# Storing the attention rows of a block in three parts of two chunks, through two half-size buffers

## The chip, the cores and the metric

The kernel runs on one core of a Trainium2 chip. The metric is the time of one execution in microseconds (us), read from the device. Five engines work side by side, each through its own program in order: PE (matrix multiplies; its weight loads are listed as PEld), DVE (vector), ACT (activations, and here also copies out of the matmul banks), POOL, and SP, which here only issues transfers. Transfers run on 16 DMA engines that all issuing engines share. Matmuls write into PSUM banks; another engine must copy ("evict") a bank before it can be written anew.

## The reference

What must be computed, cut to its core:

```python
# q, k, v: (4, 12, 448, 64); w_pre, w_post: (12, 12)
scores = scale * (q @ k.T)                       # per batch and head
scores = einsum('bhij,hg->bgij', scores, w_pre)  # mix of the heads
attn = exp(scores - max); attn /= sum + 1e-9
attn = einsum('bhij,hg->bgij', attn, w_post)     # second mix
x = (attn @ v) as rows of 768                    # 1792 rows
out = (sigmoid(x @ w_gate) * (x @ w_val)) @ w_out
```

Everything is float32. The first half (attention) makes x, the second half (a gated layer of width 1536) uses it.

## The kernel before, in words

Attention goes by blocks of 120 query rows (88 in the last block of a batch): 4 blocks in each of 4 batches, 16 in all. A block has sets of ten rows; two sets make a unit, and one unit is worked on in one **slot** of the main loop. There are 92 units, six to a block of 120 and five to a block of 88. Several units are in flight: in slot s the first mix (`premix`, line 213, PE) and the maximum (`rowmax`, line 218, DVE) are done for unit s+3, the exponential (`expo`, line 225, ACT) too, the scaling (lines 231, 237 and 243, on DVE and POOL) for unit s+1, and the second mix (`postmix`, line 255, PE, evicted by `mix`, line 263, ACT) for unit s. The scores of a later block (line 159, PE, evicted at line 165) run in between. `premix` reads a tile T that `regroup` (lines 203 and 205) loads six slots ahead, from SP; there are four T buffers and three `pm` banks, and a bank is free again when `expo` has read it.

When a block's second mix is complete, `av` (line 282, PE) multiplies it with v. The result has six chunks of 128 columns by the block's rows. Chunks 0 and 1 are made in the slot after the block, chunks 2 and 3 two slots later, chunks 4 and 5 four slots later, each at the slot's end. They go to one PSUM bank (pool `ps_av`, one buffer). After chunk 3, ACT evicts four chunks at once into `xt` (line 292), and after chunk 5 the last two. Pool `xp` holds a single `xt` buffer of four chunks, so an eviction into it waits until the store before it has landed. The stores are issued by `flush` (line 271) at the start of the next slot, on SP, right behind that slot's `regroup`. SP also issues the loads of k, q and v (lines 137, 145 and 172) and of raw weights for the second half (line 1037). SP's transfers take eight completion semaphores in turn, so each one waits until the transfer eight places ahead of it has landed.

The last two blocks differ: chunks 4 and 5 of the last block but one go into a spare T buffer, and the last block's six chunks are all made in one slot and evicted into the `mix` buffer that is then free, chunks 4 and 5 by way of the `mx` bank. After that the second half loads x from DRAM (line 1107) and works on its own order, which a planner fixes when the program is built; the planner doesn't know of the evictions.

Of the kernel before, what the change touches and what calls it, by code (L numbers as in the profile page):

```python
# [9 lines left out]
F32 = mybir.dt.float32  # L10
# [6 lines left out]
AF = mybir.ActivationFunctionType  # L17
# [7 lines left out]
QB = 120  # L25
# [16 lines left out]
def _attention(ctx, tc, ins, B, H, S, D, xs, raws, make_moe):  # L42

    nc = tc.nc
# [3 lines left out]
    KC = H * D // 128  # L48
# [7 lines left out]
    const = ctx.enter_context(tc.tile_pool(name="a_const", bufs=1))  # L56
    vst = ctx.enter_context(tc.tile_pool(name="a_vst", bufs=3))
    mp = ctx.enter_context(tc.tile_pool(name="a_m", bufs=1))
    xp = ctx.enter_context(tc.tile_pool(name="a_x", bufs=1))
    grp_ctx = ExitStack()  # L60
    tp, ep, pp, sm = (grp_ctx.enter_context(tc.tile_pool(name=f"a_{n}", bufs=b))
                          for n, b in (("t", 1), ("e", 3), ("p", 2), ("s", 4)))
# [6 lines left out]
    ps_av = ctx.enter_context(tc.tile_pool(name="ps_av", bufs=1, space=PSUM))  # L69
    ps_mx = ctx.enter_context(tc.tile_pool(name="ps_mx", bufs=1, space=PSUM))  # L70
# [6 lines left out]
    def two_banks(pool, tag):  # L77
        return pool.tile([128, 2, 512], F32, tag=tag, name=tag)
# [11 lines left out]
    sw = const.tile([128, 1], F32, name="sw")  # L90
# [35 lines left out]
    NU = len(units)  # L126
    moe = make_moe(NG)
    NBK = len(blocks)
# [39 lines left out]
    vt = {}  # L168
# [22 lines left out]
    mixes = [mp.tile([128, 4, H, QB], F32, name=f"mix{i}") for i in range(2)]  # L191

    t_bufs = [tp.tile([128, 2, S], F32, name=f"T{i}") for i in range(4)]
# [73 lines left out]
    av_t, stores = {}, []  # L267

    def flush():
        while stores:  # L270
            nc.sync.dma_start(out=stores[0][0], in_=stores.pop(0)[1])

    def av(bi, c):
        b, i0, n = blocks[bi][:3]
        u, h = divmod(2 * c, QUAD)
        if c % 4 == 0:
            last = bi == NBK - 1 and c
            t = two_banks(ps_mx, "mx")[:, 0] if last else ps_av.tile([128, 512], F32, tag="av", name="av")
            av_t[bi] = t[:, :4 * QB].rearrange("p (c s) -> p c s", c=4)
        for jb in range(4):  # L280
            for i in range(2):
                nc.tensor.matmul(av_t[bi][64 * i:64 * i + 64, c % 4, :n], lhsT=vt[b, u][:, h + i, jb, :],  # L282
                                 rhs=mixes[bi % 2][:, jb, 2 * c + i, :n], start=(jb == 0), stop=(jb == 3))
        if c % 4 == 3 or c == KC - 1:
            c0 = c - c % 4
            if bi == NBK - 1:
                xt = mixes[1 - bi % 2][:, c // 4, :4][:, :c + 1 - c0, :n]
            elif bi == NBK - 2 and c0:
                xt = t_bufs[NU % len(t_bufs)][:, 0, :(c + 1 - c0) * n].rearrange("p (c s) -> p c s", s=n)
            else:  # L290
                xt = xp.tile([128, 4, QB], F32, tag="xt", name="xt")[:, :c + 1 - c0, :n]
            nc.scalar.activation(out=xt, in_=av_t.pop(bi)[:, :c + 1 - c0, :n], func=AF.Copy, scale=sw)
            stores.append((xs[b, c0:c + 1, :, i0:i0 + n].rearrange("c p s -> p c s"), xt))
            if bi == NBK - 1:
                flush()

# [14 lines left out]
    for b in range(B):  # L311
# [3 lines left out]
        s = f + 5  # L315
        for i in range(H // 2):
            s = max(s + 1, f + 6 + 2 * (2 * i // QUAD))
# [16 lines left out]
    for bi in range(NBK):  # L334
        s0 = first[bi + 1]
        s1 = first[bi + 2] if bi + 2 < len(first) else s0
        for c in range(KC):
            at(min(s0 + c // 2 * 2, s1), av, bi, c)
            if bi == NBK - 1:
                at(s1, moe.between, c)  # L340
# [63 lines left out]
    for s in range(min(min(plan), -LEAD), max(plan) + 1):  # L404
# [25 lines left out]
        if 0 <= s + 1 < NU:  # L430
            p_lo(s + 1)
        tail = (av, moe.between, moe.early)
        if s == NU - 1:
            nc.scalar.activation(out=iw, in_=sw, func=AF.Sigmoid)
# [774 lines left out]
@with_exitstack  # L1209
def kernel(ctx, tc, B, H, S, D, ins, out):  # L1210
    nc = tc.nc
    top = ctx.enter_context(tc.tile_pool(name="top", bufs=1))
    dram = ctx.enter_context(tc.tile_pool(name="dram", bufs=1, space=DRAM))
    xs = dram.tile([B, H * D // 128, 128, S], F32, name="xs")
    with tc.manual_schedule():
        raws = top.tile([128, 13 * H * D // 2], F32, name="raws")
        with ExitStack() as c2:
            moe = _attention(c2, tc, ins, B, H, S, D, xs, raws,
                             lambda NG: _Moe(tc, xs, ins, out, raws, NG, top))
        moe.run()  # L1220
# [72 lines left out]
```

## Time and profile before

| | us |
|---|---|
| median of three executions | 796.8 (796.78 to 797.81) |
| the profiled execution | 798.64 |
| its span, first to last instruction | 796.9 |
| PE busy in the span | 770.0 (97%) |
| ACT busy in the span | 566.9 (71%) |

Attention fills the span up to about 365 us; what follows is the gated layer. All rows come from the one profiled execution; its span, 796.9, is 1.7 us below its own time and stands at the median of the other executions. A matmul's end is modelled by the profile, so that a PE that shows no idle time can still be slowed by its clock; the granted clock, in parts of full speed, is listed with each stretch.

### The profile page before, as it was taken

The page shows a single profiled execution, that of the slowest core. Times are in us where ns is not written, and L with a number is a line of the kernel's source. Part 1 is how long each engine was busy: PE and PEld are TensorE (multiplying, and loading weights), DVE is VectorE, ACT ScalarE, POOL GpSimd, SP SyncE. Part 2 cuts the span into 40 slices and gives each one's busy share as a digit, 9 for nine tenths or more (in the row PEclk, how much of TensorE's full clock was granted, in tenths as well). Part 3 has the DMA queues.
Part 4 walks back from the last instruction along what each step waited for, and adds up shares of the span by engine and source line. Part 5 has one row for each costly group of instructions (what it writes and reads, how often), then busy time and mean ns, then how long its engine had stood idle before and what let it go on. Part 6 is the DMA issues. An engine that isn't in the chain of part 4 may idle for free.

```text
span 796.9 us, 23624 instructions
## 1 busy us (share of the span) xinstructions
PE 770.0 (97%) x9626; PEld 425.7 (53%) x9626; DVE 631.9 (79%) x1092; ACT 566.9 (71%) x1122; POOL 253.6 (32%) x426
## 2 busy tenths in 40 slices
PE   8999999999979999968999999999999999999998
PEld 2465666566646666654555555555555555555554
DVE  4996899799958998789998989679786899997111
ACT  3897989898968899777886867668766784563000
POOL 1563547454534455420213122223322222010000
PEclk9999999999989999979999999999999999999999
DMA  5776678747875475636615374665657788995001
GB/s 187 253 239 214 206 236 262 260 153 237 256 231 188 158 234 192 233 109 231 204 55 195 131 243 169 247 201 187 210 162 272 279 310 300 381 355 222 35 35 69
DMA packets 80716, 166.16 MB, mean 209 GB/s; under 512 B 20448, under 2 KB 57664, under 8 KB 80608
## 3 DMA queue, kind: packets, MB, share of 16 engines
q1 hardware_dynamic: 72304, 132.88, 50.3%
q0 software_dynamic: 7728, 31.27, 10.2%
q8 instruction: 75, 1.23, 0.6%
q10 hardware_dynamic: 576, 0.51, 0.2%
q14 instruction: 33, 0.27, 0.1%
HBM read 87.77 MB, written 38.15 MB: 158 GB/s over the span
## 4 chain that ended last, share of the span: by engine, by line
PE 80%; ACT 6%; DMA 5%; DVE 5%; POOL 2%; issue 1%; SPq 1%; ACTq 0%; DVEq 0%; POOLq 0%
PE bank L1147 32%; PE bank L1158 18%; PE pm L213 9%; PE qk L159 8%; PE av L282 7%; PE mx L255 6%; ACT e L225 2%; DVE m L1131 2%; ACT mix L263 2%; DMA T<-st 2%; DMA m<-xs 1%; DMA xs<-xt 1%; DVE pl L243 1%; DVE nm L218 1%; ACT st L165 1%
## 5 line engine op out<-in xcount | busy, mean ns | idle before, releaser
L1147 PEld LDWEIGHTS <-m 128*128 128x128 f16 x1512 | 147.5, 98 | 142.3 <-DVE m L1131 4.1
L1147 PE MATMUL bank<-m,m 128*128 128x448 f16 x1116 | 214.4, 353 | 3.3 <-DVE m L1131 3.2
L237 POOL TENSOR_SCALAR ph<-e,ss 128x448 f16<-128x448 f32 x180 | 112.6, 638 | 158.3 <-DVE ss L231 114.4
L225 ACT ACTIVATE e<-pm,nm 128x448 f32<-128x448 f32 x180 | 115.2, 641 | 30.3 <-DVE nm L218 27.9
L218 DVE TENSOR_REDUCE nm<-pm 128x1 f32<-128x448 f32 x180 | 103.3, 614 | 32.7 <-PE pm L213 29.5
L213 PE MATMUL pm<-T,w 64*64 64x448 f32 (+1 forms) x720 | 110.1, 564 | 7.8 <-ACT e L225 5.4
L243 DVE SCALAR_TENSOR_TENSOR pl<-e,ss,ph 128x448 f16<-128x448 f32 x180 | 115.8, 683 | 2.0 <-POOL ph L237 2.0
L1158 PEld LDWEIGHTS <-m 128*128 128x128 f16 x756 | 73.9, 98 | 69.1
L159 PE MATMUL qk<-k,q 64*64 64x448 f32 x736 | 103.8, 549 | 3.2 <-ACT st L165 2.0
L263 ACT ACTIVATE mix<-mx 128x960 f32<-128x960 f32 (+1 forms) x92 | 104.4, 1135 | 1.5 <-PE mx L255 1.5
L255 PEld LDWEIGHTS <-ph 64*128 64x128 f16 x2880 | 64.5, 94 | 72.1 <-issue 40.3
L1158 PE MATMUL bank<-m,m 128*128 128x448 f16 x468 | 92.9, 353 | 0.0
L282 PE MATMUL av<-mix,v 128*64 128x120 f32 (+1 forms) x1504 | 86.0, 269 | 0.0
L255 PE MATMUL mx<-w2hi,ph 64*128 64x60 f16 x1440 | 72.2, 190 | 7.0 <-ACT mix L263 5.2
L1147 PE MATMUL bank<-m 128*128 128x448 f16 x396 | 77.9, 353 | 0.1
L282 PEld LDWEIGHTS av<-mix,v 128*64 128x64 f32 x1504 | 76.0, 141 | 2.7 <-issue 0.4
L255 PE MATMUL mx<-w2hi,pl 64*128 64x60 f16 x1440 | 71.4, 189 | 0.5 <-DVE pl L243 0.5
L255 PE MATMUL mx<-w2lo,ph 64*128 64x60 f16 x1440 | 71.3, 189 | 0.0
L1084 POOL CAST raws<-raws 128x768 f16<-128x768 bf16 x28 | 31.0, 1108 | 119.9 <-ACT raws L1078 119.7
L1078 ACT ACTIVATE raws<-raws 128x768 int16<-128x768 int8 (+1 forms) x72 | 60.1, 835 | 10.8 <-POOL raws L1084 10.6
L165 DVE COPY st<-qk 120x448 f32<-120x448 f32 (+1 forms) x92 | 56.5, 614 | 11.5 <-PE qk L159 11.5
L1174 DVE TENSOR_TENSOR m<-bank,m 128x448 f32<-128x448 f32 x72 | 44.5, 620 | 23.8 <-PE bank L1147 15.6
(127 smaller groups left out, 1056.7 us busy)
## 6 DMA issues: line engine op xcount, KB each, us to landing
T<-st SPq DMA_DIRECT2D x176, 210.0 KB
m<-w SPq DMA_DIRECT2D x60, 384.0 KB
raws<-in_w_dram SPq DMA_DIRECT2D x28, 767.6 KB
hs<-m POOLq DMA_DIRECT2D x48, 224.0 KB, 3.0
m<-hs SPq DMA_DIRECT2D x15, 672.0 KB
w<-m POOLq DMA_DIRECT2D x21, 384.0 KB, 4.5
w<-raws POOLq DMA_DIRECT2D x20, 384.0 KB, 4.7
v<-in_vb_dram SPq DMA_DIRECT2D x12, 512.0 KB
```

Of the source, the lines that this page charges most:

```text
L159: nc.tensor.matmul(sc[e][s0:s1, :S], lhsT=q[c][rows, s0:s1], rhs=k[rows, :], start=True, stop=True)
L165: (nc.vector.tensor_copy if e else nc.scalar.copy)(st_t[bi][:n, 2 * c + e], sc[e][:n, :S])
L213: nc.tensor.matmul(pm[bank][64 * x:64 * x + 64, :S], lhsT=w1[rows], rhs=T[rows, x], start=True, stop=True)
L218: nc.vector.tensor_reduce(nm[:, i:i + 1], pm[bank][:, :S], axis=AX.X, op=ALU.max, negate=True)
L225: nc.scalar.activation(out=e_t[u][:, i], in_=pm[units[u][2][i]][:, :S], func=AF.Exp, bias=nm_t[u][:, i:i + 1], scale=1.0, accum_out=ss_t[u ...
L237: nc.gpsimd.tensor_scalar(ph[:, i], e_t[u][:, i], ss_t[u][:, i:i + 1], 1.0, op0=ALU.mult, op1=ALU.mult)
L243: nc.vector.scalar_tensor_tensor(pl[:, i], e_t[u][:, i], ss_t[u][:, i:i + 1], p_t[u][0][:, i], op0=ALU.mult, op1=ALU.subtract)
L255: nc.tensor.matmul(mx[:, x, i, jb * HK:(jb + 1) * HK], lhsT=p[rows, i, JB[jb]:JB[jb] + 128], rhs=w[rows], start=(k == 0), stop=(k == 2))
L263: nc.scalar.activation(out=out.rearrange("p g (y r) -> p y g r", r=HALF), in_=mx_t.pop(u), func=AF.Copy, scale=1.0 / (P_UP * W_UP))
L282: nc.tensor.matmul(av_t[bi][64 * i:64 * i + 64, c % 4, :n], lhsT=vt[b, u][:, h + i, jb, :], rhs=mixes[bi % 2][:, jb, 2 * c + i, :n], start ...
L1147: self.nc.tensor.matmul(self.f32(bank), lhsT=w[a][:, k], rhs=x[b][:, k], start=self.START[i] and k == r == 0, stop=k == self.KH - 1 and r ...
L1158: self.nc.tensor.matmul(self.f32(bank), lhsT=w[a][:, k], rhs=b[bb], start=self.START[i] and j == k == r == 0, stop=j == OUT_TILES - 1 and ...
```

## The change

Each block is evicted three times, two chunks at a time, as soon as the two are made. Pool `xp` has two buffers of two chunks instead of one of four; the bytes are the same, and so is the space. The spare T buffer is no longer used for the last block but one. The last block takes chunks 2 and 3 as well by way of `mx`, one of its two banks each for chunks 2 and 3 and for 4 and 5. Evictions become 48 instead of 32, stores too; each has half the rows of chunks of the large one before.

```diff
-    xp = ctx.enter_context(tc.tile_pool(name="a_x", bufs=1))
+    xp = ctx.enter_context(tc.tile_pool(name="a_x", bufs=2))
...
-        if c % 4 == 0:
+        if c % 2 == 0:
+            if bi == NBK - 1 and c == 2:
+                av_t["last"] = two_banks(ps_mx, "mx")
             last = bi == NBK - 1 and c
-            t = two_banks(ps_mx, "mx")[:, 0] if last else ps_av.tile([128, 512], F32, tag="av", name="av")
-            av_t[bi] = t[:, :4 * QB].rearrange("p (c s) -> p c s", c=4)
+            t = av_t["last"][:, c // 2 - 1] if last else ps_av.tile([128, 512], F32, tag="av", name="av")
+            av_t[bi] = t[:, :2 * QB].rearrange("p (c s) -> p c s", c=2)
         for jb in range(4):
             for i in range(2):
-                nc.tensor.matmul(av_t[bi][64 * i:64 * i + 64, c % 4, :n], lhsT=vt[b, u][:, h + i, jb, :],
+                nc.tensor.matmul(av_t[bi][64 * i:64 * i + 64, c % 2, :n], lhsT=vt[b, u][:, h + i, jb, :],
                                  rhs=mixes[bi % 2][:, jb, 2 * c + i, :n], start=(jb == 0), stop=(jb == 3))
-        if c % 4 == 3 or c == KC - 1:
-            c0 = c - c % 4
+        if c % 2:
             if bi == NBK - 1:
-                xt = mixes[1 - bi % 2][:, c // 4, :4][:, :c + 1 - c0, :n]
-            elif bi == NBK - 2 and c0:
-                xt = t_bufs[NU % len(t_bufs)][:, 0, :(c + 1 - c0) * n].rearrange("p (c s) -> p c s", s=n)
+                xt = mixes[1 - bi % 2][:, c // 2, :2, :n]
             else:
-                xt = xp.tile([128, 4, QB], F32, tag="xt", name="xt")[:, :c + 1 - c0, :n]
-            nc.scalar.activation(out=xt, in_=av_t.pop(bi)[:, :c + 1 - c0, :n], func=AF.Copy, scale=sw)
-            stores.append((xs[b, c0:c + 1, :, i0:i0 + n].rearrange("c p s -> p c s"), xt))
+                xt = xp.tile([128, 2, QB], F32, tag="xt", name="xt")[:, :, :n]
+            nc.scalar.activation(out=xt, in_=av_t.pop(bi)[:, :, :n], func=AF.Copy, scale=sw)
+            stores.append((xs[b, c - 1:c + 1, :, i0:i0 + n].rearrange("c p s -> p c s"), xt))
```

What SP issues around the first block of the third batch stands so before (T is `regroup`'s load, k, q and raws are loads for later work, xs<-xt the store; x2 means two in a row):

```order
L203 DMA T_173<-st 120x1x448 x2
L137 DMA k<-in_kp_dram 128x448
L1037 DMA raws<-in_w_dram 128x1533
L203 DMA T_170<-st 120x1x448 x2
L137 DMA k<-in_kp_dram 128x448 x2
L145 DMA q<-in_qp_dram 128x720
L203 DMA T_171<-st 120x1x448 x2
L271 DMA xs<-xt 128x4x120
L137 DMA k<-in_kp_dram 128x448
L203 DMA T_172<-st 120x1x448 x2
L203 DMA T_173<-st 120x1x448 x2
L271 DMA xs<-xt 128x2x120
```

and now, from the same place (lines behind the change count one less):

```order
L203 DMA T_173<-st 120x1x448 x2
L271 DMA xs<-xt 128x2x120
L137 DMA k<-in_kp_dram 128x448
L1036 DMA raws<-in_w_dram 128x1533
L203 DMA T_170<-st 120x1x448 x2
L137 DMA k<-in_kp_dram 128x448 x2
L145 DMA q<-in_qp_dram 128x720
L203 DMA T_171<-st 120x1x448 x2
L271 DMA xs<-xt 128x2x120
L137 DMA k<-in_kp_dram 128x448
```

One store more stands in front of the loads of two units, and the store behind them is half as large.

ACT's order in the same block is this before (e is `expo`, mix and xt are evictions, v_abs and raws are work for the second half), from the first mix after chunks 0 and 1:

```order
L178 ACTIVATE v_abs,vm<-v 128x512
L225 ACTIVATE e,ss<-pm_117,nm 128x448
L165 COPY st<-qk 90x448
L263 ACTIVATE mix_169<-mx 128x4x48x5
L225 ACTIVATE e,ss<-pm_115,nm 128x448
L998 ACTIVATE raws,abs_w_141<-raws 128x384
L225 ACTIVATE e,ss<-pm_116,nm 128x448
L165 COPY st<-qk 90x448
L263 ACTIVATE mix_169<-mx 128x4x48x5
L225 ACTIVATE e,ss<-pm_117,nm 128x448
L292 ACTIVATE xt<-av,sw 128x480
```

and this now:

```order
L178 ACTIVATE v_abs,vm<-v 128x512
L291 ACTIVATE xt<-av,sw 128x240
L225 ACTIVATE e,ss<-pm_117,nm 128x448
L165 COPY st<-qk 90x448
L263 ACTIVATE mix_169<-mx 128x4x48x5
L225 ACTIVATE e,ss<-pm_115,nm 128x448
L997 ACTIVATE raws,abs_w_141<-raws 128x384
L225 ACTIVATE e,ss<-pm_116,nm 128x448
L165 COPY st<-qk 90x448
L263 ACTIVATE mix_169<-mx 128x4x48x5
L225 ACTIVATE e,ss<-pm_117,nm 128x448
L291 ACTIVATE xt<-av,sw 128x240
```

The small eviction of chunks 0 and 1 is new, ahead of the next slot's `expo`, and the large one has become small. On PE, DVE and POOL the instructions stand in the same order as before.

## Rows read from the trace of the kernel before

**Rows 1.** The page: busy time by engine, and the last-ending chain by engine.

```profile
PE 770.0 (97%) x9626; PEld 425.7 (53%) x9626; DVE 631.9 (79%) x1092; ACT 566.9 (71%) x1122; POOL 253.6 (32%) x426
...
PE 80%; ACT 6%; DMA 5%; DVE 5%; POOL 2%; issue 1%; SPq 1%; ACTq 0%; DVEq 0%; POOLq 0%
```

**Rows 2.** Waits of the span: who waited for whom, us, times, longest.

```profile
ACT xt L292 <- DMA xs<-xt: 9.2, 4, 4.8
...
PE pm L213 <- DMA T<-st: 2.4, 3, 1.3
```

**Rows 3.** ACT's timeline, 54 to 233: start, us, instruction, idle before and what ended it.

```profile
54.38 0.68 ACT L292 ACTIVATE xt<-av,sw 128x480 f32<-128x480 f32 x1
54.92 0.66 ACT L225 ACTIVATE e<-pm,nm 128x448 f32<-128x448 f32 x1
...
63.59 0.46 ACT L292 ACTIVATE xt<-av,sw 128x240 f32<-128x240 f32 x1 [2.07 <-DMA xs<-xt]
63.95 0.63 ACT L225 ACTIVATE e<-pm,nm 128x448 f32<-128x448 f32 x1
...
145.90 0.46 ACT L292 ACTIVATE xt<-av,sw 128x240 f32<-128x240 f32 x1 [1.45 <-DMA xs<-xt]
...
206.07 0.41 ACT L292 ACTIVATE xt<-av,sw 128x176 f32<-128x176 f32 x1 [0.83 <-DMA xs<-xt]
...
219.13 0.65 ACT L292 ACTIVATE xt<-av,sw 128x480 f32<-128x480 f32 x1
...
232.66 0.46 ACT L292 ACTIVATE xt<-av,sw 128x240 f32<-128x240 f32 x1 [4.83 <-DMA xs<-xt]
```

**Rows 4.** SP's timeline, the same stretch: T loads and stores as they are issued.

```profile
54.50 2.24 SPq L203 DMA_DIRECT2D T<-st  x2
56.85 0.43 SPq L271 DMA_DIRECT2D xs<-xt  x1
...
213.74 1.69 SPq L203 DMA_DIRECT2D T<-st  x2
...
224.68 0.44 SPq L271 DMA_DIRECT2D xs<-xt  x1
```

**Rows 5.** PE's timeline: the matmuls of attention with the long idle times before them.

```profile
64.72 0.60 PE L213 MATMUL pm<-T,w 60*64 60x448 f32 x3 [1.39 <-ACT e L225]
...
147.46 0.60 PE L213 MATMUL pm<-T,w 60*64 60x448 f32 x3 [1.19 <-ACT e L225]
...
154.18 0.98 PE L159 MATMUL qk<-k,q 64*64 64x448 f32 x8 [0.77 <-ACT st L165]
...
221.49 0.97 PE L213 MATMUL pm<-T,w 64*64 64x448 f32 x4 [0.80 <-DMA T<-st]
...
231.15 0.93 PE L213 MATMUL pm<-T,w 64*64 64x448 f32 x2 [1.26 <-DMA T<-st]
234.22 1.02 PE L213 MATMUL pm<-T,w 60*64 60x448 f32 x3 [2.14 <-ACT e L225]
```

**Rows 6.** Stretches: length, busy by engine; the last three are PEclk, DMA share, GB/s.

```profile
64.70:70.00 5.30, 5.28 (x88) 3.37 (x90) 2.97 (x5) 5.30 (x12) 0.88 (x3) 0.68 0.71 244
146.00:150.00 4.00, 2.81 (x65) 1.37 (x66) 2.40 (x6) 4.00 (x11) 1.44 (x3) 1.00 0.61 212
220.00:224.00 4.00, 2.90 (x64) 1.23 (x58) 2.49 (x6) 3.96 (x11) 2.46 (x6) 1.00 0.95 264
234.20:240.00 5.80, 5.78 (x78) 3.54 (x80) 3.24 (x6) 4.99 (x11) 1.42 (x3) 0.53 0.54 182
```

**Rows 7.** The last-ending chain in order of time: start, us, piece.

```profile
56.85 6.65 DMA xs<-xt
...
214.66 8.05 DMA T<-st
```

**Rows 8.** The hand-over to the second half, on SP and on ACT.

```profile
366.34 1.66 SPq L1099 DMA_DIRECT2D m<-w  x3
...
370.31 1.12 ACT L1126 ACTIVATE m<-m,one_w 128x384 f16<-128x384 f32 x2 [1.81 <-DMA m<-w]
```

## The prediction

> **What bounds the kernel now.** The page comes first. PE is busy for 97% of the span, and the chain that ended last runs through PE for 80% of it, through ACT for 6% and through transfers for 5% [rows 1]. So an edit off PE pays only where PE stands still or runs slowly. The waits view says where the edited lines stand still: ACT waits four times, 9.2 us in all, for a store of x to land before it can evict into the same buffer [rows 2]. ACT's timeline dates the four at 63.59 (2.07 us), 145.90 (1.45), 206.07 (0.83) and 232.66 (4.83) [rows 3]. Each is the second eviction of a block, and three of them are those of the first block of a batch, when SP also loads k, v, q and raw weights.
>
> Next is what PE makes of them. Its timeline has idle time for ACT right behind three of the four: 1.39 us before 64.72, 1.19 before 147.46 with 0.77 more before 154.18, and 2.14 before 234.22 [rows 5]. No such row stands behind the third. The stretches view adds the clock: behind the first and the fourth the granted clock falls to the lower of its levels, 1.2 instead of 2.4 GHz, for part of 64.7 to 70.0 (mean 0.68) and of 234.2 to 240.0 (0.53), while it stays at 1.00 behind the second [rows 6]. PE is busy in both stretches and gets less done: 5.30 x 0.32 = 1.70 us and 5.80 x 0.47 = 2.73 us.
>
> So the four waits cost PE 1.39 + 1.70 = 3.09, then 1.19 + 0.77 = 1.96, then 0, then 2.14 + 2.73 = 4.87 us: 9.92 together. That is the most that the change can give back, and it is a different sum from the 9.2 us that ACT waited.
>
> The waits view also names what comes next: PE waited for T loads three times, 2.4 us in all [rows 2], all of it at 221.49 to 231.15 [rows 5], right ahead of the fourth wait. A T load took 8.05 us there and a store 6.65 us at the first wait [rows 7], with the DMA engines 95% busy at 264 GB/s [rows 6].
>
> **The four waits.** With two buffers an eviction waits for the store two evictions back. Chunks 4 and 5 now reuse the buffer of chunks 0 and 1, four slots earlier; the tightest reuse, around a block of 88, is three slots, where it was two before. The longest way from an eviction to a free buffer in the trace is 219.13 to 232.66, less than 13.5 us: the store was issued at 224.68, 5.5 us behind its eviction [rows 3, 4], and then landed. Four slots there last about as long, and the store of chunks 0 and 1 is issued well before that, behind the T load of 213.74. I take all four waits as gone.
>
> **The new evictions on ACT.** From one start to the next a large eviction takes 54.92 - 54.38 = 0.54 us of ACT and a small one 63.95 - 63.59 = 0.36 [rows 3]. A block costs 3 x 0.36 = 1.08 instead of 0.90, so 0.18 more, and 16 blocks cost 2.9. Most of it is covered by ACT's idle time, as it is busy for 71% of the span [rows 1]; where ACT ends the chain it is paid. The chain's 6% is 48 us, about seven blocks' worth of slots of 3.5 us. Two of them lie at the first two waits and are charged there; for the other five I take 5 x 0.18 = 0.9 us. The bounds are 0 and 13 x 0.18 = 2.3, without the three blocks at the waits that count. The small eviction of chunks 0 and 1 waits for PE's `av` at its slot's end, and the `expo` behind it waits for a `premix` that PE runs after that `av`, so nothing that could run is held up.
>
> The trace's rows split an eviction into 0.18 us fixed and 0.18 us per two chunks. The Trainium skill (ScalarE: Activation LUTs, Rules for kernel authors) has about 0.3 us per ACTIVATE and 0.83 ns per element, which is an estimate of 0.50 us for the small one, against 0.36 here; five blocks would then cost 1.5 us and not 0.9, and the total would be 0.6 us later.
>
> PE is not held by the `av` bank: chunk 2 needs the eviction of chunk 1, which stands on ACT ahead of the `mix` that PE's next `postmix` needs anyway.
>
> **The extra stores on SP.** A block's bytes and rows are the same, so the engines carry no more. But one small store now stands ahead of the loads of two units. With half the large store's 240 KB in front, those loads land 120 KB / 264 GB/s = 0.47 us later, if the queue is full [rows 6]. If instead the eight places in flight are the limit, a place is worth 8.05 / 8 = 1.0 us [rows 7]. I take the first, because the engines are 95% busy there, and keep 0 and 1.0 as bounds. It counts only where T is late or nearly so. At the fourth wait T is late already (1.26 us before 231.15) and all of 0.5 is paid. At the first, the load issued at 54.50 and 2.24 later, at some 6 to 8 us, lands around 62 to 64, just when PE gets to its use before 64.72 [rows 4, 5]: 0.5. At the second I take 0.2. Elsewhere T has several us in hand, since no other row shows PE waiting for it. At the third wait ACT gains 0.83 us, but PE gets sooner to the late T load of 221.49; I book 0.
>
> **The end of attention.** The last block's three evictions cost ACT 0.2 us more than its two did, by the same arithmetic. They stand in a stretch where ACT and DVE prepare the second half. The last store is ahead of the weight loads issued at 366.34, for which ACT waited 1.81 us at 370.31 [rows 8]. So 0.2 us later goes through to the end. The bounds are 0 and 0.5.
>
> **The sum.** First wait 3.09 - 0.18 - 0.5 = 2.4; second 1.96 - 0.18 - 0.2 = 1.6; third 0; fourth 4.87 - 0.5 = 4.4; other blocks -0.9; end -0.2. Together 7.3 us. Nothing later takes it back: the second half starts from what attention delivers and has no time of its own. The profiled span of 796.9 becomes 789.6, and with the same 1.7 us outside it as before the profiled execution 791.3; the median of 796.8 becomes 789.5.
>
> **Rivals.**
>
> *The T loads take the place of the stores.* For it: PE's three waits for T stand right ahead of the fourth wait. A T load later by a full place, 1.0 us, makes PE's idle time before 231.15 as long as 2.26 us. That is over the 2.14 us behind which the clock fell, and 2.73 is paid again. Fourth wait: 4.87 - 1.0 - 2.73 = 1.1; first 3.09 - 0.18 - 1.0 = 1.9; second 1.96 - 0.18 - 0.3 = 1.5; with -0.9 and -0.2 together 3.4, so 793.4. Against it: the 1.10 us of idle time at 220 to 224 left the clock at 1.00 [rows 6], and the bytes are the same.
>
> *The waits stay.* If stores are so late that the buffer of two evictions back is busy too, ACT waits as before. That needs a store over 10 us behind its eviction at a block of 88, or 14 elsewhere. Only 219.13 to 232.66 comes near. The time would be 796.8, within 0.2% (1.6 us, about what a measurement of this kernel can tell from no change).
>
> *Slower: the sixteen extra transfers cost the T chain.* Each takes one of SP's eight places, at up to 8.05 / 8 = 1.0 us. It decides once an extra store costs PE more than 9.92 / 16 = 0.6 us on average. If all sixteen cost 1.0 it gives back 9.92, pays 16 and the 1.1 above: 796.8 + 7.2 = 804. Against it: T is late in one stretch alone, and in most blocks there is no queue. The Trainium skill (DMA: Bandwidth & Descriptors, Anatomy of one DMA) speaks for this rival, with a fixed cost of about 2.0 us per transfer on the path it describes; the rows here show the time from issue to landing in a full queue, not that cost by itself.
>
> *More than I book.* Neither T nor ACT costs anything: 796.8 - 9.9 = 786.9.
>
> **How the numbers follow.** Forecast, 787 to 792: 0.62. T takes the place, 792 to 795: 0.20. No change: 0.08. Slower: 0.06. More than booked, below 787: 0.04. Faster by over 0.2% is 0.62 + 0.20 + 0.04 = 0.86, the same 0.08, slower 0.06. A range from 787.0 to 794.5 holds the first case and nearly all of the second, 0.8.
>
> **What would show it.** The row of ACT waiting for xs<-xt gone from the waits; PE's idle time before the counterparts of 64.72, 147.46 and 234.22 below 0.5 us; the granted clock at 1.00 in the stretches that answer to 64.7 to 70.0 and 234.2 to 240.0; waits for T at 221 to 231 up by about half a us; 48 evictions of about 0.36 us of ACT each. It is wrong if ACT still waits for stores, if PE waits for T by 3 us more than before, or if the low clock comes back at 231.

## The result, and the profile after

The changed kernel takes 789.5 us (median of six executions, 788.07 to 791.1) against 796.9 us for the kernel before, measured beside it: a ratio of 0.9911, with a 95% interval of 0.9890 to 0.9931. That is 7.4 us less, by the interval 5.5 to 8.8. The prediction had said 789.5, in a range of 787.0 to 794.5. So the total was right. Not all of its terms were, and what follows asks how far each was.

The page of the profiled execution (789.52 us, span 787.7): busy time by engine, then the last-ending chain. They answer to [rows 1].

```profile
PE 764.9 (97%) x9626; PEld 425.7 (54%) x9626; DVE 631.7 (80%) x1092; ACT 569.0 (72%) x1138; POOL 257.3 (33%) x426
...
PE 79%; ACT 9%; DVE 4%; DMA 3%; issue 2%; POOL 2%; SPq 1%; ACTq 0%; DVEq 0%; POOLq 0%
```

PE's 9626 matmuls take 5.1 us less busy time (770.0 before), at least in part as fewer of them run at the low clock. ACT has 16 instructions more and 2.1 us more of work. Transfers make up 3% of the chain instead of 5%.

The waits view answers to [rows 2]; these are ACT's and PE's lines that matter. The row of ACT waiting for xs<-xt, 9.2 us in four times, is not in it any more.

```profile
ACT xt L291 <- PE av L284: 5.2, 2, 2.7
...
PE av L284 <- issue: 1.8, 1, 1.8
...
PE pm L213 <- DMA T<-st: 0.7, 2, 0.4
```

ACT's two waits for PE stand at none of the four places. ACT's timeline shows the evictions that take the places of the four in [rows 3], and the two waits, at 216.88 and 347.03:

```profile
61.29 0.48 ACT L291 ACTIVATE xt<-av,sw 128x240 f32<-128x240 f32 x1
...
141.09 0.48 ACT L291 ACTIVATE xt<-av,sw 128x240 f32<-128x240 f32 x1
...
200.52 0.44 ACT L291 ACTIVATE xt<-av,sw 128x176 f32<-128x176 f32 x1
...
216.88 0.46 ACT L291 ACTIVATE xt<-av,sw 128x240 f32<-128x240 f32 x1 [2.52 <-PE av L284]
225.65 0.49 ACT L291 ACTIVATE xt<-av,sw 128x240 f32<-128x240 f32 x1
...
347.03 0.46 ACT L291 ACTIVATE xt<-av,sw 128x240 f32<-128x240 f32 x1 [2.66 <-PE av L284]
```

All four (61.29, 141.09, 200.52, 225.65) start without a wait. The wait at 216.88 lies behind a stop of PE itself, at 213.51 below. The wait at 347.03 is no new one; the kernel before has it at the same eviction, of the last block but one:

```profile
356.18 0.46 ACT L292 ACTIVATE T<-av,sw 128x240 f32<-128x240 f32 x1 [2.42 <-PE av L282]
```

PE's timeline answers to [rows 5]:

```profile
69.33 0.98 PE L159 MATMUL qk<-k,q 64*64 64x448 f32 x8 [0.96 <-ACT st L165]
...
142.64 1.34 PE L213 MATMUL pm<-T,w 64*64 64x448 f32 x6 [0.49 <-ACT e L225]
...
149.75 0.98 PE L159 MATMUL qk<-k,q 64*64 64x448 f32 x8 [0.43 <-ACT st L165]
...
213.51 0.72 PE L284 MATMUL av<-mix,v 128*64 128x120 f32 x6 [1.85 <-issue]
...
226.55 1.65 PE L213 MATMUL pm<-T,w 64*64 64x448 f32 x6 [0.33 <-DMA T<-st]
```

And the stretches (length; busy by engine; the last three are PEclk, DMA share, GB/s) answer to [rows 6]:

```profile
62.20:67.50 5.30, 5.30 (x118) 3.55 (x114) 4.44 (x9) 5.30 (x14) 2.58 (x3) 1.00 0.71 243
139.60:142.70 3.10, 2.61 (x70) 1.30 (x67) 2.11 (x5) 3.10 (x10) 1.44 (x3) 1.00 0.80 270
211.30:213.60 2.30, 0.45 (x13) 0.22 (x6) 2.30 (x5) 2.05 (x5) 2.22 (x3) 1.00 0.84 254
213.60:217.00 3.40, 3.40 (x35) 3.10 (x39) 0.33 (x2) 0.89 (x4) 2.18 (x5) 0.51 0.78 240
226.50:232.60 6.10, 6.05 (x105) 3.63 (x108) 4.67 (x10) 6.10 (x16) 1.44 (x3) 1.00 0.76 233
```

The two stretches with a mean clock of 0.68 and 0.53 before, 64.7 to 70.0 and 234.2 to 240.0, have 1.00 at their counterparts. PE's idle times of 1.39, 1.19 and 2.14 us are gone or below 0.5. The 0.77 us before 154.18 has become 0.43, and 0.96 us before 69.33 is new. And a stretch is there that no term of the prediction has: PE stands still for 1.85 us before 213.51, released by nothing that the profile shows, and runs at the lower clock for the 3.4 us behind. By the prediction's own way of counting that is 1.85 + 3.40 x 0.49 = 3.5 us given back.

So the terms have to be measured one by one. The starts of `premix` on PE (its first matmul of a unit) cut attention into stretches. The table has the length of each in us, for both profiles of either kernel (the second ones are the runs "before_again" and "repeat" below):

| stretch, from the premix of one unit to that of another | before | before, again | after | after, again | mean gain | forecast |
|---|---|---|---|---|---|---|
| 15 to 17, first wait | 11.52 | 9.78 | 8.74 | 8.55 | 2.0 | 2.4 |
| 37 to 40, second wait | 12.97 | 15.05 | 11.78 | 11.79 | 2.2 | 1.6 |
| 55 to 61, third wait and the late T loads | 24.76 | 24.03 | 24.73 | 25.48 | -0.7 | -0.5 |
| 61 to 64, fourth wait | 17.44 | 17.32 | 13.21 | 14.14 | 3.7 | 4.9 |
| the rest of units 0 to 91 | 254.22 | 254.96 | 253.18 | 254.98 | 0.5 | -0.9 |
| from unit 91 to the end | 458.82 | 458.71 | 458.87 | 457.26 | 0.7 | -0.2 |

(The prediction's 4.4 for the fourth wait stands here as 4.9 for the wait and -0.5 for the T load, which comes ahead of unit 61.) The stretch ahead of unit 0 is within 0.5 us in all. The mean gain of the spans is 8.4 us (796.9 and 796.7 against 787.7 and 789.0). The three waits that counted gave 7.9 together, where 8.9 was forecast. Two profiles of one kernel differ by up to 2.1 us in a single row, so that a mean gain of less than a us is not told from none.

The last row's 0.7 is the clock of one execution. Over the 35 us behind the `premix` of unit 91 the mean clock is 0.85 in three of the four profiles and 0.90 in "repeat", and 0.05 of 35 us is 1.75. The changed kernel's two:

```profile
328.80:363.80 35.00, 26.43 (x391) 18.65 (x388) 30.38 (x39) 27.64 (x44) 5.62 (x10) 0.85 0.45 135
```

```profile
331.70:366.70 35.00, 25.84 (x393) 18.07 (x392) 31.98 (x44) 28.44 (x44) 5.59 (x10) 0.90 0.49 152
```

### The profile page after: what moved, and what is told of

Same layout as the page of the kernel before. It is cut to its first block, busy times and chain, and to the rows that moved or that the text cites. A ratio compares the mean times of both kernels' runs of the same rounds, so it can differ in the third digit from the quotient of the medians.

```text
span 787.7 us, 23686 instructions
## 1 busy us (share of the span) xinstructions
PE 764.9 (97%) x9626; PEld 425.7 (54%) x9626; DVE 631.7 (80%) x1092; ACT 569.0 (72%) x1138; POOL 257.3 (33%) x426
## 3 DMA queue, kind: packets, MB, share of 16 engines
q8 instruction: 75, 1.23, 0.6%
## 4 chain that ended last, share of the span: by engine, by line
PE 79%; ACT 9%; DVE 4%; DMA 3%; issue 2%; POOL 2%; SPq 1%; ACTq 0%; DVEq 0%; POOLq 0%
PE bank L1146 33%; PE bank L1157 18%; PE pm L213 8%; PE av L284 7%; PE qk L159 7%; PE mx L255 6%; ACT e L225 3%; ACT mix L263 2%; DVE m L1130 2%; ACT m L1125 1%; ACT st L165 1%; DVE nm L218 1%; DMA T<-st 1%; DMA k<-in_kp_dram 1%; POOL ph L237 1%
## 5 line engine op out<-in xcount | busy, mean ns | idle before, releaser
L225 ACT ACTIVATE e<-pm,nm 128x448 f32<-128x448 f32 x180 | 115.6, 643 | 27.4 <-DVE nm L218 24.2
L213 PE MATMUL pm<-T,w 64*64 64x448 f32 (+1 forms) x720 | 105.4, 561 | 1.6 <-ACT e L225 0.8
L159 PE MATMUL qk<-k,q 64*64 64x448 f32 x736 | 99.9, 540 | 4.0 <-ACT st L165 3.0
L1173 DVE TENSOR_TENSOR m<-bank,m 128x448 f32<-128x448 f32 x72 | 44.6, 620 | 24.2 <-PE bank L1146 16.0
```

The source lines that it names most:

```text
L159: nc.tensor.matmul(sc[e][s0:s1, :S], lhsT=q[c][rows, s0:s1], rhs=k[rows, :], start=True, stop=True)
L213: nc.tensor.matmul(pm[bank][64 * x:64 * x + 64, :S], lhsT=w1[rows], rhs=T[rows, x], start=True, stop=True)
L225: nc.scalar.activation(out=e_t[u][:, i], in_=pm[units[u][2][i]][:, :S], func=AF.Exp, bias=nm_t[u][:, i:i + 1], scale=1.0, accum_out=ss_t[u ...
```

## Experiments

### A second profile of either kernel

> The kernel before once more, for a second profile, since the prediction's four waits come from one execution. Theory: ACT's four waits for stores are there again at the same evictions, 7 to 11 us in all, and PE loses 8 to 12 us behind them and in the two low-clock stretches; the time is 797 within 1 us. Rival (the waits belong to the one execution): fewer than three of them, or at other blocks, below 5 us in all.

Measured: 798.1 us, a ratio of 1.0013 (0.9985 to 1.0041) to itself. ACT's waits and PE's for `expo`:

```profile
ACT xt L292 <- DMA xs<-xt: 7.0, 4, 2.9
...
PE pm L213 <- ACT e L225: 4.9, 4, 2.0
```

Four waits again, at the same four evictions: 1.27, 2.64, 0.24 and 2.88 us, 7.0 in all (9.2 in the first profile). The prediction's base was no accident of one execution, but the size of each wait is one: the second is 2.64 here and was 1.45, the fourth 2.88 and was 4.83. The time is 0.1 us above what was expected.

The clock moved too. PE's idle times behind the first and the second wait, and the stretches behind them:

```profile
64.16 0.60 PE L213 MATMUL pm<-T,w 60*64 60x448 f32 x3 [0.59 <-ACT e L225]
...
147.13 0.96 PE L213 MATMUL pm<-T,w 60*64 60x448 f32 x3 [1.96 <-ACT e L225]
```

```profile
64.10:69.50 5.40, 5.34 (x106) 3.37 (x110) 3.03 (x8) 5.40 (x13) 1.44 (x3) 1.00 0.70 246
147.10:150.70 3.60, 3.56 (x34) 1.44 (x36) 1.45 (x3) 3.60 (x10) 0.19 (x1) 0.53 0.65 226
232.50:239.50 7.00, 5.53 (x74) 3.31 (x76) 3.67 (x8) 6.20 (x14) 1.44 (x3) 0.51 0.65 219
```

In the first profile the clock was low behind the first wait and at 1.00 behind the second [rows 6]; here it is the other way round. Behind the second wait that costs 3.60 x 0.47 = 1.7 us, as the first wait's low clock did (1.70). So most of what sets the two profiles apart in the table's first two rows (1.74 less and 2.08 more) is where the low clock fell. Behind the fourth wait it is low in both.

> The changed kernel once more, for a second profile. In its first one PE stood still for 1.85 us before 213.51, after the first of 32 av matmuls, with no releaser named, and the clock was low for 3.4 us behind it. If that belongs to the order of the work (a buffer, a load, a bank), it is there again at the same matmul with the same length. If it belongs to the one execution (the program itself arriving late on PE), it is gone or stands elsewhere, and the span is shorter by up to 1.85 us and the 1.7 us of the low clock, 784 to 787.7. The median stays at 789.5 either way.

Measured: 790.73 us, ratio 0.9921 (0.9897 to 0.9946), span 789.0 in the profile. PE's waits for T and without a releaser:

```profile
PE pm L213 <- DMA T<-st: 2.5, 2, 1.8
...
PE pm L213 <- issue: 1.7, 1, 1.7
PE mx L255 <- issue: 0.3, 1, 0.3
PE av L284 <- issue: 0.2, 1, 0.2
```

The stop of 213.51 is not there at that length. One of 1.75 us stands some 4 us earlier, ahead of a `premix` (209.55), with a small one of 0.19 at the counterpart of the first (215.05). So it is hardly the `av` bank or a load of v that PE waits for: it moves between executions of one kernel. The span did not get shorter, as there is also a wait for T of 1.77 us at 227.91, and the low clock came behind that one:

```profile
227.91 1.90 PE L213 MATMUL pm<-T,w 64*64 64x448 f32 x6 [1.77 <-DMA T<-st]
```

```profile
209.50:213.00 3.50, 3.45 (x75) 1.94 (x78) 2.40 (x5) 1.66 (x4) 0.23 (x2) 1.00 1.06 259
...
227.90:234.00 6.10, 6.09 (x92) 3.33 (x93) 3.21 (x7) 4.24 (x10) 1.45 (x3) 0.72 0.77 244
```

(The two fences are PE's timeline and the stretches view of this run.) Behind 1.75 us of idle time the clock stayed at 1.00, behind 1.77 us it fell to the lower level for part of the stretch. The length of the stop alone doesn't tell.

### Is it the wait, or the smaller stores?

Two kernels take the change apart. The first leaves the large and the small eviction as they were and gives the small one a buffer of its own:

```diff
+    xq = stg_ctx[(NB - 3) % ST].enter_context(tc.tile_pool(name="a_x2", bufs=1))
...
-                xt = xp.tile([128, 4, QB], F32, tag="xt", name="xt")[:, :c + 1 - c0, :n]
+                own = c0 and bi < NBK - 3
+                xt = (xq if own else xp).tile([128, 2 if own else 4, QB], F32, tag="xt", name="xt")[:, :c + 1 - c0, :n]
```

> The kernel before, with one thing added: the small eviction (chunks 4 and 5) of the first thirteen blocks has a buffer of its own, so that it no longer waits for the store of chunks 0 to 3. Evictions stay 32, stores too, nothing is split. Theory (the gain is the removal of ACT's four waits, and the halves are only the way to find the space): it gains what the changed kernel gains and is spared the sixteen extra evictions and stores. By the prediction's sum that is 9.9 off, 787.0 (786 to 788.5); if the extra evictions and stores cost nothing, as the profile of the changed kernel suggests, it stands level with it at 789.5 (788.5 to 790.5). Rival (the gain comes from the smaller, earlier stores): it stays within 3 us of the kernel before, 794 to 797.

The second keeps the three evictions and takes the second buffer away:

```diff
-    xp = ctx.enter_context(tc.tile_pool(name="a_x", bufs=2))
+    xp = ctx.enter_context(tc.tile_pool(name="a_x", bufs=1))
```

> The changed kernel with a single buffer of two chunks. Everything else is as in the changed kernel: 48 evictions, 48 stores of half the size. Now each eviction waits for the store two slots earlier. Theory (the wait for the buffer is what costs): ACT waits for stores in the same crowded stretches as before, for chunks 2 and 3 as well as for 4 and 5, so the gain is lost: 795 to 803, with a row of ACT waiting for xs<-xt of 8 us or more. Rival (the smaller and earlier stores are what helps): 788 to 791 and no such row above 2 us.

Measured beside "repeat": buffers of their own 788.67 us, 0.9903 (0.9868 to 0.9938); one half buffer 796.27 us, 0.9992 (0.9964 to 1.0019). The first has no row of ACT waiting for xs<-xt; the second has:

```profile
ACT xt L291 <- DMA xs<-xt: 6.7, 4, 2.4
```

That is less than the 8 us that was expected, and only two of its four waits stand in the stretches of the table (2.37 us at 144.14 and 1.54 at 229.33; the others are at 193.10 and 276.31). But it is the same kind of wait, and with it the time of the kernel before. The gain belongs to the second buffer. Cutting the eviction in three gives nothing by itself; it is what makes room for two buffers in the same space. The own buffers' time is that of the second case expected, level with the changed kernel (788.5 to 790.5). Their median is 2.1 us below that of "repeat" beside it, which would just fit the 2.3 us that the prediction had booked for more evictions, more stores and the end (0.9 + 1.2 + 0.2), but the intervals overlap, and no more can be said.

### What do an eviction and a store cost?

> The changed kernel with each eviction made as two, of one chunk each: 48 more instructions on ACT, the same stores, buffers and bytes. Theory (an eviction's fixed part is covered by ACT's idle time everywhere, since the stretches of the changed kernel without waits were no longer than before in spite of 16 more evictions): 789 to 791.5, level with the changed kernel. Rival (the prediction's way of booking: 0.18 us for each in five blocks of sixteen, here three more in each of them, and 0.5 at the end): 2.7 + 0.5 = 3.2 us later, 793 to 794. If each were paid in full, 48 x 0.18 = 8.6 us later, 799.

```diff
-            nc.scalar.activation(out=xt, in_=av_t.pop(bi)[:, :, :n], func=AF.Copy, scale=sw)
+            acc = av_t.pop(bi)
+            for y in range(2):
+                nc.scalar.activation(out=xt[:, y], in_=acc[:, y, :n], func=AF.Copy, scale=sw)
```

Measured: 790.0 us, 0.9914 (0.9886 to 0.9942), level with the changed kernel. The rival's 793 to 794 lies at and above the upper end of the interval (0.9942 x 797.67 = 793.0). Forty-eight more evictions cost nothing that can be seen. What the times leave room for is 0.0052 x 797 = 4.1 us (from the lower end of the changed kernel's interval, 0.9890, to the upper end here), 0.09 us for each, so that the sixteen of the change cost 1.4 us at the most by this.

> The changed kernel with each store issued as two, of one chunk each: 48 more transfers on SP, the same bytes, evictions and buffers. Theory (bytes in front of the T loads count, places in SP's queue don't): within 1.5 us of the changed kernel, 788 to 791. Rival (each place in SP's queue is worth 8.05 / 8 = 1.0 us where the queue is full): 3 stores for each of the four blocks in crowded stretches at 1.0 us, 12 us later, about 801; if each of the 48 costs it, 837.

```diff
-            stores.append((xs[b, c - 1:c + 1, :, i0:i0 + n].rearrange("c p s -> p c s"), xt))
+            for y in range(2):
+                stores.append((xs[b, c - 1 + y, :, i0:i0 + n], xt[:, y]))
```

Measured: 791.43 us, 0.9939 (0.9914 to 0.9964), 0.7 us above "repeat" in the same series, with intervals that overlap. Even from the lower end of the one to the upper end of the other it is 0.0067 x 797 = 5.3 us, 0.11 us for each of 48 stores as a mean. The full place of 1.0 us, and the 0.6 us from which the prediction's slower rival decides, are out. The mechanism of that rival can be seen all the same, in the profiled execution, which at 795.37 us is the slowest of its twelve:

```profile
PE pm L213 <- DMA T<-st: 6.9, 4, 2.5
```

PE waited 6.9 us for T in this execution, where the changed kernel's two have 0.7 and 2.5. The stretch from unit 55 to 61 is 27.89 us here.

### Could the waits have been removed otherwise?

The kernel before with two lines exchanged, so that a slot's stores are issued ahead of its T loads:

```diff
-        next_dma = rows_until(s + LEAD, next_dma)
         flush()
+        next_dma = rows_until(s + LEAD, next_dma)
```

> The kernel before, with the stores issued ahead of the two T loads of the slot instead of behind them; one large buffer, 32 evictions, nothing split. Theory (ACT's four waits are as long as they are because a store stands in SP's queue behind T loads, up to 5.5 us behind its eviction): the fourth wait falls from 4.83 to about 2.2 us, the others of 2.07, 1.45 and 0.83 to nothing, and most of the changed kernel's gain is had with a swap of two lines: 789.5 to 792.5. Rival (the store waits for one of SP's eight places wherever it stands, so it lands no sooner): the waits stay, 795 to 799. Second rival (SP now waits for ACT's eviction ahead of the T loads): PE's waits for T grow above 6 us, 797 or more.

Measured: 791.26 us, 0.9926 (0.9901 to 0.9951): as good as the change within what the intervals tell. SP's timeline at the fourth wait, and the waits of ACT and PE:

```profile
222.22 0.38 SPq L271 DMA_DIRECT2D xs<-xt  x1
223.02 1.67 SPq L203 DMA_DIRECT2D T<-st  x2
```

```profile
ACT xt L292 <- DMA xs<-xt: 4.5, 2, 2.3
...
PE pm L213 <- DMA T<-st: 1.3, 2, 1.1
```

The store of 224.68 [rows 4] is issued at 222.22, 2.5 us sooner, and ACT waits 2.16 us where it had 4.83. This execution too is the slowest of its kernel, 794.07 us. The waits at the first and the third place are gone. The one at the second place is not shorter (2.35 us), against what was expected, and yet the stretch from unit 37 to 40 took 12.01 us, some 0.2 more than in the changed kernel. PE's waits for T, 1.3 us against 2.4 and 2.3, show no harm to the T loads from being one place further back.

> The changed kernel with the stores of the first fifteen blocks issued by POOL, behind the scaling of the slot, so that they take no place in SP's queue (the few stores of the bounds of v go with them). Theory (PE's remaining waits for T in the crowded stretches, 0.3 to 2.5 us in two profiles, come from what SP has queued ahead of a T load, a half store among it): 0.5 to 2 us faster than the changed kernel, 787.5 to 790. Rival (the engines carry the same bytes, T loads land no sooner, and POOL pays for issuing): 790 to 793, with POOL's scaling later and PE waiting for ph or pl in the slots behind a store.

```diff
-    def flush():
+    def flush(eng=nc.sync):
         while stores:
-            nc.sync.dma_start(out=stores[0][0], in_=stores.pop(0)[1])
+            eng.dma_start(out=stores[0][0], in_=stores.pop(0)[1])
...
         next_dma = rows_until(s + LEAD, next_dma)
-        flush()
...
             scale(s + 1)
+        flush(nc.gpsimd)
```

Measured: 791.31 us, 0.9923 (0.9897 to 0.9948). Taking the stores out of SP's queue gains nothing; PE's waits for T are 1.3 us in its profile, between the changed kernel's two.

### The stops without a releaser

What is PE waiting for when the profile names nothing? The records of transfers have an instruction queue beside the queues for data. On the page of the changed kernel:

```profile
q8 instruction: 75, 1.23, 0.6%
```

75 packets are 1.23 MB, 16 KB each. Between 25 and 345 us of the fourteen profiles their starts are 4.8 to 6.5 us apart in the middle half, and 7 us or more in 124 cases of 758. At the stop of the changed kernel one ran from 203.59 to 204.61 and the next from 211.03 to 212.06, 7.4 us later; PE went on at 213.51. At the stop of "repeat": 199.30, then 207.11 to 208.21, and PE went on at 209.55. Over the two profiles of before and after and the twelve of the experiments, PE has 28 stops of more than 0.25 us without a releaser ahead of 600 us, and in all 28 it goes on 1.26 to 1.71 us behind the end of such a packet, which came 5.5 to 8.9 us after the one before it. That overlaps with the usual distance, so it is not the distance alone that makes a stop. They also stand at fixed places of PE's program: counted in matmuls from the start, at 599, 1362, 2379, 2507, 4287 and 4415 for instance, whole multiples of 127.2 apart (763, 1017, 128, 1780, 128), and so are all 28, to within two matmuls. Of the 773 times that PE passes such a place between 25 and 345 us in the fourteen profiles, the packet had ended 2.8 to 4.3 us ahead in the middle half, and under 2 us ahead in some 95. One reading fits all of this, though no row names it: PE waits for the next piece of its own program.

What makes a packet late was put to a test by moving transfers away:

> The changed kernel with four loads of raw weights (192 KB each) moved six slots ahead, from about 199 to 213 us, where the DMA engines are 94% busy, to about 178 to 192, where they are 61 to 71% busy. All bytes are the same. Theory (PE's stops without a releaser at 205 to 230 us come when a packet of the program's own queue is late among these transfers: the packets are 5 to 6 us apart elsewhere, and 7.4 to 8.3 us apart right ahead of every such stop): no stop of over 0.3 us without a releaser at 195 to 230 us and no low clock there, 2 to 4 us faster than the changed kernel, 786 to 788. Rival (the stops belong to the executions and not to the crowd): they stand as in the changed kernel, 789 to 791, or move with the loads.

```diff
-            at(EARLY_AT[k] + slot, moe.early, k, step)
+            at(EARLY_AT[k] + slot - (6 if k == 6 and step < 4 else 0), moe.early, k, step)
```

Measured: 789.98 us, 0.9910 (0.9882 to 0.9937). The profile has no such stop at 195 to 230 us and the clock is at 1.00 there; one of 0.79 us stands at 45.94 instead, and T waits are 2.6 us. The time isn't the 786 to 788 of the theory. With buffers of their own as well:

> The kernel before with a buffer of its own for the small eviction, and with four loads of raw weights six slots earlier. If the two are worth what their profiles suggest (no extra store or eviction, less of a crowd at 195 to 215 us), 786 to 788.5, the fastest here; if the stops of PE only move from one crowded stretch to another, level with each alone, 788.5 to 790.5.

Measured: 789.63 us, 0.9912 (0.9879 to 0.9946), and in the profile, the slowest of seven executions at 794.39 us, five stops of 0.34 to 2.29 us, one of them at 199.74. The stops move, and nothing was won. No kernel here beats the changed one by more than the intervals allow.

The opposite, adding transfers where none of the earlier profiles had a stop:

> The changed kernel with twelve transfers of 224 KB added, DRAM to DRAM, two in each of the slots 38 to 43, issued by ACT (the work that they do is of no use to anything). They fall at about 155 to 178 us, where the DMA engines were 44 to 76% busy and no profile shows a stop of PE without a releaser. Theory (a crowd of transfers is what makes a packet of the program late): there is such a stop in this stretch, right behind a packet that comes 6.5 us or more after the one ahead of it, or the packets' lead over PE falls below 2 us from the usual 3 to 5; time 790 to 795. Rival (the stops have another cause): packets every 5 to 6 us and a lead of 3 us or more all through the stretch, no stop; whatever time is lost is then lost to T.

```diff
         flush()
+        for x in range(2 if 38 <= s < 44 else 0):
+            nc.scalar.dma_start(out=ins["crowd"][s - 38, x], in_=kp[x, s - 38])
```

Measured: 796.52 us, 0.9993 (0.9970 to 1.0017). Most of it is ACT, which stood still ahead of the last two of the added transfers and ran its next instruction after 6.18 us (the expectation of the next run has 5.25):

```profile
180.68 0.63 ACT L225 ACTIVATE e<-pm,nm 128x448 f32<-128x448 f32 x1 [6.18 <-DMA q<-in_qp_dram]
```

One packet came 1.89 us ahead of PE's use of it (174.98), below the 2 us that the theory had named as its sign, the others 2.9 to 4.0; PE had no stop in the stretch. With fewer and larger transfers:

> The crowd again, without what held ACT in it: only eight added transfers, two in each of the slots 40 to 43, of 448 KB each, DRAM to DRAM, issued by ACT (their work is of no use to anything). In the run with twelve, ACT stood for 5.25 us at the eleventh, and the time says nothing on the program's packets. In two profiles of the changed kernel the packets ended 3.2 to 4.5 us ahead of PE's use of them at 155 to 190 us. Theory (a crowd makes them late): a lead below 2 us or a stop of PE without a releaser at 160 to 195 us, and 790 to 795. Rival (another cause): a lead of 3 us or more throughout; the time 790.5 or what T loads cost beyond it.

Measured: 803.16 us, 1.0070 (1.0045 to 1.0095), slower. ACT stood still for even longer; its timeline, with ACTq for the transfers that it issues:

```profile
165.57 0.50 ACTq L407 DMA_DIRECT2D crowd<-in_kp_dram  x1
167.48 0.81 ACTq L407 DMA_DIRECT2D crowd<-in_kp_dram  x1
...
176.72 5.26 ACTq L407 DMA_DIRECT2D crowd<-in_kp_dram  x2
182.37 0.63 ACT L225 ACTIVATE e<-pm,nm 128x448 f32<-128x448 f32 x1 [10.42 <-DMA crowd<-in_kp_dram]
```

What held ACT is in the trace: each of the added transfers waits on one of the eight completion semaphores that SP's transfers use in turn. In this run's chain the fifth waits for a T load that SP had issued, and the sixth for the landing of the fifth:

```profile
166.28 10.42 DMA T<-st
176.72 4.74 DMA crowd<-in_kp_dram
```

In the run with twelve, a load of q that SP had issued ends the wait.

The packets came 3.5 to 4.4 us ahead in this stretch, as ever, but for one that came while PE stood (12.8 us ahead). The one packet with a short lead, in the run with twelve, is all that speaks for the crowd; neither run shows a stop by it, and both held ACT, and so PE, before the crowd could last. What delays a packet stays open.

## Why the prediction was right, point by point

**The four waits as gone** was right, in either profile. "One half buffer" shows that it is the second buffer that does it, and "buffers of their own" that nothing else of the change is needed.

**First and fourth wait** (2.4, and 4.9 ahead of the T load's 0.5): the mechanism was right, the low clock included, which was over half of either loss in the profile that the prediction used: the clock is at 1.00 in the counterparts of [rows 6]. The first profiles give 2.8 and 4.2, the means of two 2.0 and 3.7. The terms were sized by one execution. In the other one of the kernel before, the clock stayed at 1.00 behind the first wait, and the stretch is 1.7 us shorter.

**Second wait** (1.6): 1.2 by the profile that the prediction used, 2.2 as a mean, as the low clock stood behind this wait in the other profile. And 0.77 of its 1.96 us, the idle time before 154.18, was counted as the wait's without a sign that it was: 0.43 and 0.72 us of it are there in the changed kernel's two profiles (149.75 and 150.34).

**Third wait** (0, and the late T loads behind it): the stretch lost 0.7 us as a mean where -0.5 was booked, but for another reason. The prediction had PE get sooner to a late T load and wait there longer. In the changed kernel's first profile PE waits 0.3 us for T at 226.55, and not 0.5 more than the 2.1 us of 221.49 and 231.15 [rows 5]. What took the time was the stop without a releaser: 1.85 and 1.75 us in the two profiles, the first with 1.7 us of low clock behind it; in the second, 1.77 us of waiting for T came on top. In the ten other kernels, none of which has the wait at the third place, the stretch varies with such stops and waits. Four take 21.4 to 22.5 us (buffers of their own, more evictions, stores on POOL, one half buffer), "own_and_earlier" 23.1, four 24.2 to 24.3 and "single stores" 27.9, where before it was 24.0 and 24.8. So "I book 0" came out near the mark by luck: one profile of each kernel leaves open what the third wait itself was worth, and something that the trace of before didn't show took what there was.

**T loads later by 0.5** (1.2 in all with the other two places): not seen as forecast. PE's waits for T are 0.7 and 2.5 us against 2.4 and 2.3 before, a spread that hides half a us. The bounds of 0 and 1.0 for a store's place were too wide upward: 48 more stores cost 0.11 us each at the most, as a mean.

**More evictions on ACT** (-0.9) and **the end** (-0.2): probably mis-sized; no cost shows. The rest of units 0 to 91 is 0.5 us shorter as a mean, 48 further evictions leave the time where it was, and from unit 91 to the end the kernels differ by 0.05 us in the first two profiles. A cost of 1.1 us in all is not ruled out by this. The prediction took the chain's 6% on ACT as seven blocks in which 0.18 us more would be paid. But 48 us are about 14 slots of 3.5 us, and a block has five or six, so these are seven blocks only if two slots stand for one. And ACT's place on the chain says that it ended last there, not that its idle time elsewhere in the slot couldn't take 0.18 us; that last point is argued and not measured.

So the sum was right partly by luck, because errors cancelled, as far as two profiles of each kernel can tell. Against the table's means the prediction booked 2.3 us too much for the other blocks and the end (0.5 + 0.9 + 0.7 + 0.2), and 0.6 too little for the second wait; on the other side stand 0.4 and 1.2 us too much gain at the first and the fourth wait, and 0.2 at the third. That nets 1.1 us, the 8.4 of the two pairs of profiles against the 7.3 of the sum; the medians say 7.4.

**The rivals.** That waits stay is out. That extra transfers make it slower is out at its price. That the T loads take the stores' place was the best of them: its mechanism shows in "repeat", where a T wait of 1.77 us stands at the counterpart of 231.15 with the low clock behind it, and the stretch from 61 to 64 is 0.9 us longer than in the first profile. That is one of the prediction's own signs of being wrong, the low clock back at 231, and one of two profiles met it. It wasn't the rule, and 790.73 us is not the 793.4 that it would have given.

On the two pages cited: the Trainium skill (ScalarE: Activation LUTs, Rules for kernel authors) would have made the evictions dearer, 0.6 us later in all. The estimate of 0.50 us from it is near the 0.46 to 0.49 us that an eviction of 128x240 itself takes in the rows; from one start to the next it was 0.34 us in the changed kernel. In the kernel's time no run here shows the difference, as 48 more evictions cost nothing that can be measured. The Trainium skill (DMA: Bandwidth & Descriptors, Anatomy of one DMA) has a fixed cost of about 2.0 us per transfer on the path that it describes. "Single stores" shows that no such cost adds up along SP's queue, with 0.11 us per store at the most as a mean.

## What to carry to other kernels

Look for an engine that waits to reuse a buffer until a store from it has landed: a second, smaller buffer, or the store issued ahead of loads that have time in hand, removes the wait or shortens it, and either gave about 6 to 8 us of 797 here. Size such a term from more than one execution where it can be had: each of the four waits differed by 0.6 to 2 us between two profiles of one kernel, and the low clock, worth 1.7 us, stood behind the first wait in one and behind the second in the other. Count the clock with the idle time. And don't take it as given that an engine's 0.2 us more of work is paid because the chain passes through it.

## What the runs showed that was not expected

PE seems to stand still for its own program: 28 stops of 0.3 to 2.3 us in fourteen profiles, each ended 1.26 to 1.71 us behind a 16 KB packet of the instruction queue, at places that are multiples of 127 matmuls apart. The reading is argued from this agreement; no run made or removed such a stop at will. Such a stop is listed as "issue", moves between executions, and can bring the lower clock behind it (0.51 over 3.4 us).

An engine that issues transfers can be held by those of another: ACT stood for 10.42 us when it came to the fifth of its transfers of 448 KB, as its semaphore was still that of a T load from SP, and for 6.18 us with the last two of twelve of 224 KB.

Two idle times of PE of nearly equal length, 1.75 and 1.77 us, had the clock at 1.00 behind the one and 0.72 as a mean behind the other. The prediction's rival had taken 2.14 us as a length behind which the clock falls. But it fell behind 1.39 us [rows 5, 6] and stayed at 1.00 behind the longest of the 28 stops, 2.29 us in "own_and_earlier" (PE's timeline, then the stretch behind it):

```profile
76.32 1.66 PE L283 MATMUL av<-mix,v 128*64 128x120 f32 x28 [2.29 <-issue]
```

```profile
76.30:82.00 5.70, 5.68 (x108) 3.44 (x107) 3.01 (x6) 2.93 (x6) 1.17 (x3) 1.00 0.63 201
```

The length of one stop doesn't decide it.
